# Batch 0's k maximum by TensorE, half of q times kv on another PSUM ring, an uneven last cut, and new lists of order, engines and loads

## The chip, the cores and the metric

The kernel runs on one core of one Trainium2 chip. The metric is the device time of one launch in microseconds, as the median of several runs. 0.2% of it is 0.48 us.

## What is computed

Eight batches of eight heads with 576 tokens and 64 values per head go through "efficient" attention, and the result (4608 tokens of 512 values) through a multiplicative feed-forward network. All arrays are float32.

```
q_s = softmax(q, axis=-1)           # over the 64 values of a token
k_s = softmax(k, axis=2)            # over the 576 tokens; the maximum is over tokens too
kv  = einsum('bhsd,bhse->bhde', k_s, v)          # 64 x 64 for each head
x   = einsum('bhsd,bhde->bhse', q_s, kv)         # transposed to (4608, 512)
out = ((x @ w1) * (x @ w2) @ w3) @ w_out   # 512 -> 1024 -> 1024 -> 512
```

## The kernel before, in words

**The fold.** w3 @ w_out is formed once on the chip as `W3O`, in eight slices `ft`: `w3t` (L445) is eight TensorE transposes of 128x128 into a bank of the PSUM ring "pab", `w3T` copies them to SBUF, `pf.ft.0` and `pf.ft.1` (L457) are four matmuls of 512 columns each with the two halves of w_out (loads `wo.0`, `wo.1`) into a bank of the ring "po", and `W3O.ft` scales the sum out. Slices 4 and 5 share one load `w3.4`, 6 and 7 share `w3.5`; the others have one each (`w3.0` to `w3.3`).

**Attention of a batch b.** q: `qmx` (maximum over a token's values, L582), `qsub` (L587), `qexp` (L595), `qsm` (sum, L600), `qeps`, `qrc` (L612), `qn` (normalized q, fp16, L619), each in two parts of the tokens; then q is transposed, by TensorE (`qt`, L634, and a copy `qT`) in the first batches or by a DMA (`qd`, L642). k: `kmx` (L498 to L501) takes the maximum over a partition's own nine tokens by a tree of DVE operations. The tokens of a head lie over 64 partitions, so the maximum over them comes next: `cba` (a 32x32 stream transpose of DVE, L505, and a reduction, L508), `cbx` (four small ACT copies that bring the other 32 partitions' values across, L514) and `cb` (a reduction, L518, and a transposing spread, L520). `ksub` (L524) subtracts it, `kexp` (L532) takes the exponential. `kv` (L549, L559) multiplies k_s and v, `kve` and `kv2` (L566 to L575) divide by the sums. `xm.b.0`, `xm.b.1` and `xt.b` (L667) multiply q and kv: 512 tokens in two halves of the heads, and the 64 tokens left over; `xs` and `xts` copy them out as x in fp16.

**The network in chunks c.** Chunk c = 0 to 7 has batch c's first 512 tokens, chunk 8 the 8 x 64 left over. `up.1.c.sub.u` and `up.0.c.sub.u` (L784) are four matmuls for x @ w2 and x @ w1 each; `bs` copies the first out of PSUM, `ab` (L799, DVE) multiplies it with the second; `down.c.tb` (L806, eight matmuls of 512 columns) multiplies with `W3O`, `os` copies to SBUF and `st` stores. Chunks 0 and 1 are done in two halves of 256 tokens, and in chunk 0 each load of 256 columns of w1 and w2 is used as it comes. In chunk 8 the last quarter `down.8.3` (L821) is cut in columns, so that its copies and stores begin sooner.

**What sets the order.** Three PSUM rings of banks hold the products: "pab" (4), "po" (2), "att" (2). All steps are written out in the list `ORDER`; each engine executes its own in that order, and waits where data, a bank or a buffer are not there. `PICKS` names the engine for those steps that have a choice. `FILL` names steps ahead of which matmuls on zeros (L352) are put. Loads stand in three lists: `HW` (batch 0's q, on SP's queue), `LOADS` (on POOL's queue, at most eight outstanding: each load waits until the one eight places ahead has landed) and `LATE` (on SP again, after `w1.3` of `LOADS`). The rings and pools are declared so:

```
pab_pool = ctx.enter_context(tc.tile_pool(name="pab", bufs=4, space=bass.MemoryType.PSUM))
po_pool = ctx.enter_context(tc.tile_pool(name="po", bufs=2, space=bass.MemoryType.PSUM))
att_pool = ctx.enter_context(tc.tile_pool(name="att", bufs=2, space=bass.MemoryType.PSUM))
```

Of the kernel before, what the change touches and what calls it, by code (L numbers as in the profile page):

```python
# [10 lines left out]
F32 = mybir.dt.float32  # L11
# [6 lines left out]
class Plan:  # L18
# [59 lines left out]
q.0.1 qmx.0.1 qsub.0.1 qexp.0.1 q.0.0 ident w3.4 w3t.5 qmx.0.0 qsm.0.1 wo.0 wo.1 w3.2 k.0 w3.0 w3.3  # L78
w3.5 w3t.4 w3T.5 w3.1 w3T.4 qeps.0.1 qsub.0.0 qrc.0.1 qexp.0.0 qn.0.1 v.0 pf.5.0 pf.4.0 pf.5.1 w3t.2
qsm.0.0 k.1 w2.0 w3T.2 W3O.5 q.1.0 qt.0.16 qt.0.8 qT.0.8 pf.4.1 qT.0.16 qeps.0.0 qrc.0.0 qn.0.0 w1.0  # L80
pf.2.0 pf.2.1 w3t.0 W3O.2 W3O.4 w3T.0 qt.0.0 w3t.3 pf.0.0 w3T.3 w2.1 pf.0.1 pf.3.0 w3t.7 kmx.0.0
cba.0 cbx.0 w1.1 pf.3.1 W3O.0 w3T.7 w3t.1 pf.7.0 w3t.6 w1.2 w2.2 cb.0 ksub.0.1 ksub.0.0 kexp.0.1
kexp.0.0 pf.7.1 qT.0.0 kv.0 W3O.3 w3T.1 W3O.7 kve.0 pf.1.0 pf.1.1 w3T.6 kv2.0 xm.0.0 pf.6.0 pf.6.1
xs.0.0.1 kmx.1.0 xs.0.0.0 xm.0.1 xs.0.1.0 xs.0.1.1 up.1.0.0.0 bs.0.0.0 xt.0 qmx.1.0 k.2 w2.3 cba.1
cbx.1 up.0.0.0.0 up.1.0.1.0 up.0.0.1.0 W3O.1 bs.0.1.0 ab.0.0.0 up.1.0.0.1 up.0.0.0.1 w1.3 v.1
qsub.1.0 qexp.1.0 q.1.1 q.2 xts.0.0 bs.0.0.1 up.1.0.1.1 ab.0.1.0 cb.1 up.0.0.1.1 up.1.0.0.2 qsm.1.0
ksub.1.1 bs.0.1.1 ab.0.0.1 up.0.0.0.2 up.1.0.1.2 qeps.1.0 xts.0.1 qrc.1.0 qn.1.0 bs.0.0.2 ab.0.1.1
ab.0.0.2 kmx.2.0 cba.2 bs.0.1.2 kexp.1.1 up.0.0.1.2 up.1.0.0.3 up.0.0.0.3 up.1.0.1.3 bs.0.0.3 W3O.6
# [52 lines left out]
ab.8.0.1 st.6.3 os.7.0 os.7.1 down.7.2 up.0.8.0.2 up.1.8.0.3 ab.8.0.2 bs.8.0.3 up.0.8.0.3 up.1.8.0.4
up.0.8.0.4 ab.8.0.3 bs.8.0.4 ab.8.0.4 up.1.8.0.5 bs.8.0.5 up.0.8.0.5 up.1.8.0.6 bs.8.0.6 ab.8.0.5
up.0.8.0.6 ab.8.0.6 up.1.8.0.7 up.0.8.0.7 bs.8.0.7 ab.8.0.7 down.7.3 st.7.0 os.7.2 down.8.0 st.7.1
st.7.2 os.7.3 os.8.0 down.8.1 down.8.2 st.7.3 os.8.1 os.8.2 st.8.0 down.8.3.0 os.8.3.0 down.8.3
os.8.3 st.8.1 st.8.2 st.8.3.0 st.8.3
"""


FILL = {
    "begin": 17, "pf.5.0": 6,  # L150
}


PICKS = {
# [773 lines left out]
```

## Time and profile before

| what | value |
| --- | --- |
| median of 3 runs | 239.51 us (239.41 to 239.68) |
| the profiled execution | 239.21 us |
| its span, first to last instruction | 237.4 us |
| TensorE (PE) busy | 230.1 us, 97% |
| DVE, ACT, POOL busy | 180.3, 121.7, 110.0 us |
| fills (L352) | 23, 8.0 us |
| first up projection starts at | 33.49 us |

The span is that of one profiled execution; the launch's time holds 1.8 us more. Engines are PE (TensorE), PEld (its weight loads), DVE (VectorE), ACT (ScalarE), POOL (GpSimd) and SP (SyncE). Lines name an instruction by its source line, its output and inputs by the program's names. A row of a timeline is start, length, engine, line, operation, count, and in brackets the idle time of the engine ahead of it and what ended it. A row of the waits is engine, tile and line, what was waited for, and the total, count and longest in us. A row of the groups ends in busy time, mean ns of one and the idle time ahead. A row of a table by windows has, after the length, the busy us and the instructions of PE, PEld, DVE, ACT and POOL, then the granted clock, the DMA engines' busy share and GB/s.

### The profile page before, as it was taken

The numbers are of one execution on the slowest core, as the hardware profiler recorded it, in microseconds if no ns is written. First come the engines' busy times: TensorE is split into PE (matmuls) and PEld (weight loads), VectorE is DVE, ScalarE is ACT, GpSimd is POOL, SyncE is SP. The second block draws the span as 40 slices with busy tenths as digits, with TensorE's granted clock in tenths as the row PEclk, the third lists the DMA queues.
The fourth block names the chain that finished last, engine by engine and source line by source line (L and its number), as shares of the span: only waits on it lengthen the run. The fifth ranks groups of instructions, "written<-read, shape, count | busy, mean of one in ns | idle before, by whom it ended". The sixth has DMA issues, their size and how long they took to land.

```text
span 237.4 us, 4860 instructions
## 1 busy us (share of the span) xinstructions
PE 230.1 (97%) x1935; PEld 119.5 (50%) x1935; DVE 180.3 (76%) x277; ACT 121.7 (51%) x221; POOL 110.0 (46%) x73
## 2 busy tenths in 40 slices
PE   7889999999999999999999999999999999999994
PEld 2445658756856444444444444444444444444443
DVE  2998699998998999998999798679566365326640
ACT  1437854499856997777747754258405111010002
POOL 8234258469958899469673593338500000000000
PEclk9999999999999999999999999999999999999999
DMA  6999999999999998959699984250042070163053
GB/s 207 214 307 209 306 245 300 328 299 382 401 226 309 405 217 179 385 132 282 242 113 281 387 338 95 51 135 0 3 91 52 0 179 2 32 145 88 3 132 133
DMA packets 38742, 46.51 MB, mean 196 GB/s; under 512 B 17088, under 2 KB 22976, under 8 KB 38720
## 3 DMA queue, kind: packets, MB, share of 16 engines
q1 hardware_dynamic: 31184, 34.48, 50.2%
q0 software_dynamic: 7536, 11.73, 21.1%
q8 instruction: 15, 0.25, 0.4%
q14 instruction: 7, 0.06, 0.1%
HBM read 38.80 MB, written 9.44 MB: 203 GB/s over the span
## 4 chain that ended last, share of the span: by engine, by line
PE 81%; DMA 8%; DVE 5%; POOL 4%; issue 1%; ACT 0%; POOLq 0%; ACTq 0%
PE pab L784 46%; PE po L806 22%; DMA w<-in_moe_w_dram 6%; PE po L457 4%; PE po L821 3%; PE pkv L549 2%; DMA qT<-en 2%; PE xm L667 1%; DVE qm L582 1%; POOL k L524 1%; PE w3t L445 1%; POOL en L619 1%; POOL w L406 1%; DVE ab L799 1%; DVE kmx L498 1%
## 5 line engine op out<-in xcount | busy, mean ns | idle before, releaser
L784 PE MATMUL pab<-x,w1sb 128*128 128x512 f16 (+1 forms) x320 | 65.9, 337 | 0.4 <-DVE kmx L499 0.4
L784 PE MATMUL pab<-x,w2sb 128*128 128x512 f16 (+1 forms) x320 | 66.0, 337 | 0.0
L799 DVE TENSOR_TENSOR ab<-pab,bsb 128x512 f16<-128x512 f32 x72 | 48.6, 682 | 20.2 <-PE pab L784 13.6
L806 PE MATMUL po<-W3O,ab 128*128 128x512 f16 x256 | 58.9, 379 | 0.0
L784 PEld LDWEIGHTS <-w1sb 128*128 128x128 f16 x352 | 34.2, 98 | 28.5 <-DMA w1sb<-in_moe_w_dram 0.6
L784 PEld LDWEIGHTS <-w2sb 128*128 128x128 f16 x352 | 33.5, 98 | 27.5 <-issue 0.7
L325 ACT CAST bsb<-pab 128x512 f16<-128x512 f32 x46 | 26.8, 582 | 35.8 <-PE pab L784 34.6
L524 POOL TENSOR_TENSOR k<-k,cb 128x1152 f32<-128x1152 f32 x12 | 31.4, 2628 | 16.4 <-issue 5.1
L806 PEld LDWEIGHTS <-ab 128*128 128x128 f16 x256 | 24.5, 98 | 28.5 <-issue 0.4
L587 POOL TENSOR_TENSOR q<-q,qm 128x1024 f32<-128x1024 f32 (+1 forms) x14 | 29.5, 2125 | 13.1 <-DVE rc L573 5.4
L325 ACT COPY osb<-po 128x512 f32<-128x512 f32 (+1 forms) x25 | 14.3, 571 | 40.3 <-PE po L806 26.8
L619 POOL TENSOR_TENSOR en<-eq,qr 128x1024 f16<-128x1024 f16 (+1 forms) x13 | 27.2, 2106 | 10.5 <-DVE qr L612 10.4
L582 DVE TENSOR_REDUCE qm<-q 128x20 f32<-128x1280 f32 (+1 forms) x16 | 21.2, 1340 | 3.6 <-DMA q<-in_q_dram 3.6
L325 DVE CAST bsb<-pab 128x512 f16<-128x512 f32 x26 | 17.6, 677 | 6.8 <-PE pab L784 6.3
L600 DVE TENSOR_REDUCE qr<-eq 128x20 f32<-128x1280 f16 (+1 forms) x16 | 21.5, 1341 | 1.5 <-ACT eq L595 1.4
L595 ACT ACTIVATE eq<-q 128x1280 f16<-128x1280 f32 (+1 forms) x16 | 18.5, 1161 | 4.8 <-DVE q L587 3.9
L532 ACT ACTIVATE ek<-k 128x1152 f16<-128x1152 f32 x16 | 18.2, 1163 | 3.8 <-POOL k L524 3.8
L489 DVE TENSOR_REDUCE km<-k 128x128 f32<-128x1152 f32 x8 | 16.9, 2149 | 0.0
L457 PE MATMUL po<-wosb,w3T 128*128 128x512 f16 x64 | 15.3, 379 | 0.5 <-DMA wosb<-in_moe_w_out_dram 0.5
L325 DVE COPY osb<-po 128x512 f32<-128x512 f32 x12 | 8.3, 688 | 9.1 <-PE po L806 7.9
L329 ACT ACTIVATE x<-xm 128x512 f16<-128x512 f32 x18 | 10.3, 597 | 6.4 <-PE xm L667 6.2
L325 ACT CAST v<-v 128x1152 f16<-128x1152 f32 x9 | 10.3, 1148 | 0.3 <-DMA v<-in_v_dram 0.3
(70 smaller groups left out, 194.0 us busy)
## 6 DMA issues: line engine op xcount, KB each, us to landing
out_dram<-osb SPq DMA_DIRECT2D x66, 128.0 KB, 2.6
q<-in_q_dram SPq DMA_DIRECT2D x5, 1152.0 KB, 7.7
v<-in_v_dram SPq DMA_DIRECT2D x5, 1152.0 KB, 8.9
k<-in_k_dram SPq DMA_DIRECT2D x4, 1152.0 KB, 10.1
k<-in_k_dram POOLq DMA_DIRECT2D x3, 1152.0 KB, 14.1
v<-in_v_dram POOLq DMA_DIRECT2D x1, 1152.0 KB, 13.9
v<-in_v_dram SPq DMA_DIRECT2D x2, 576.0 KB, 5.9
q<-in_q_dram SPq DMA_DIRECT2D x2, 576.0 KB, 7.7
```

The lines of the kernel that those rows point to most:

```text
L325: return [(nc.scalar.copy if eng == "ACT" else engine[eng].tensor_copy)(out=out, in_=in_)]
L457: nc.tensor.matmul(st["pf", ft], lhsT=st["w3T", ft][:, gt, :], rhs=wosb[:, gt, :], start=(gt == 0), stop=(gt == N_FT - 1))
L524: return [engine[eng].tensor_tensor(out=kb[:, two(hp), :, :], in0=kb[:, two(hp), :, :], in1=st["cb", b][:, two(hp), None, :].broadcast_to( ...
L532: nc.scalar.activation(out=st["ek", b][:, hp, :, :].rearrange("p j (i d) -> p i j d", i=2), in_=kb[:, two(hp), :, :], func=AF.Exp)
L582: dve.tensor_reduce(out=st["qm", b][:, :, j], in_=qb[:, :, j, :], axis=AX.X, op=ALU.max)
L587: return [engine[eng].tensor_tensor(out=qb[:, :, j, :], in0=qb[:, :, j, :], in1=st["qm", b][:, :, j, None].broadcast_to([P, HH, n, D]), op ...
L595: nc.scalar.activation(out=st["eq", b, p], in_=qb[:, :, j, :], func=AF.Exp)
L600: dve.tensor_reduce(out=st["qr", b][:, :, slice(*PARTS[p])], in_=st["eq", b, p], axis=AX.X, op=ALU.add)
L619: return [engine[eng].tensor_tensor(out=st["en", b][:, j, :, :].rearrange("p j h d -> p h j d"), in0=st["eq", b, p], in1=st["qr", b][:, :, ...
L784: nc.tensor.matmul(st["p", one, c, sub, u][:, a * (t1 - t0):(a + 1) * (t1 - t0)], lhsT=w[:, ct, fb * P:(fb + 1) * P], rhs=x()[:, ct, t0:t1 ...
L799: dve.tensor_tensor(out=st["ab", c][:, nf * u:nf * u + nf, t0:t1], in0=cut(st["p", 0, c, sub, u]), in1=cut(st["bsb", c, sub, u]), op=ALU.mult)
L806: nc.tensor.matmul(st["po", c, tb], lhsT=st["ab", c][:, ft, tb * P:(tb + 1) * P], rhs=W3O[:, ft, :], start=(ft == 0), stop=(ft == N_FT - 1))
```

## The change

1. `PEK = [0]`: for batch 0 the maximum over partitions is no longer made by `cba`, `cbx`, `cb`. TensorE transposes the partial maxima as float32 (`kT`, two transposes with a float32 identity `ident32`), DVE reduces along the free axis (`kr`), and four float32 matmuls of 128 columns with the identity as the moving operand spread the result over 64 partitions each (`kB`). `ksub.0` reads it from PSUM, on DVE only. Other batches keep the old way.
2. From batch 3 on `xm.b.0` takes its bank from "pab" instead of "att"; `xm.b.1` stays on "po", `xt.b` on "pab".
3. The last block's cut is 320 and 192 columns instead of 256 and 256.
4. `FILL` goes from 17 at the start and 6 ahead of `pf.5.0` to 14 at the start and 8 ahead of `pf.2.0`.
5. `LOADS`, `LATE`, `ORDER` and `PICKS` are listed anew. In `LOADS`, `w3.2` and `w3.0` stand ahead of `wo.0`, and `q.1.0` ahead of `k.1`. The fp16 identity is made on POOL behind the first two loads instead of ahead of them. In `PICKS` some steps change between DVE, ACT and POOL (`qsub.0.0` goes to POOL, `ksub.1.0` to DVE, the last block's 320 columns to DVE).

```diff
 FILL = {
-    "begin": 17, "pf.5.0": 6,
+    "begin": 14, "pf.2.0": 8,
 }
...
 LOADS = [
-    ("w3", 4), ("wo", 0), ("wo", 1), ("w3", 2), ("k", 0), ("w3", 0), ("w3", 3), ("w3", 5),
-    ("w3", 1), ("v", 0), ("k", 1), ("w2", 0), ("q", 1, 0), ("w1", 0), ("w2", 1), ("w1", 1),
-    ("w1", 2), ("w2", 2), ("k", 2), ("w2", 3), ("w1", 3), ("v", 1), ("q", 1, 1),
+    ("w3", 2), ("w3", 4), ("w3", 0), ("wo", 0), ("wo", 1), ("k", 0), ("w3", 3), ("w3", 5),
+    ("w3", 1), ("v", 0), ("q", 1, 0), ("k", 1), ("w1", 0), ("w2", 0), ("w2", 2), ("w2", 1),
+    ("w1", 1), ("w1", 2), ("k", 2), ("w2", 3), ("w1", 3), ("v", 1), ("q", 1, 1),
 ]
...
+    plan.add(("ident32",), "ACT", 0.28, lambda: nc.scalar.copy(out=ident32, in_=ident16), needs=[("ident",)],
+             lead=200.0)
...
+        def kT():
+            st["kT", b] = kbank("kT")
+            for n in range(NHP):
+                nc.tensor.transpose(st["kT", b][:, n, :], st["km", b].rearrange("p h d -> p (h d)")[
+                    :, n * P:(n + 1) * P], ident32)
+
+        def kr():
+            st["kr", b] = work.tile([P, NHP, G], F32, tag="kr", name="kr")
+            dve.tensor_reduce(out=st["kr", b], in_=st["kT", b].rearrange("p n (g r) -> p n g r", g=G),
+                              axis=AX.X, op=ALU.max)
+
+        def kB():
+            st["kB", b] = kbank("kB")
+            for n in range(NHP):
+                for gg in range(G):
+                    nc.tensor.matmul(st["kB", b][gg * HALF:(gg + 1) * HALF, n, :],
+                                     lhsT=st["kr", b][:, n, gg:gg + 1].broadcast_to([P, HALF]),
+                                     rhs=ident32, start=True, stop=True)
+            if not b:
+                st["cb", b] = st["kB", b].rearrange("p n (i d) -> p (n i) d", d=D)
...
-            return "pab" if name[0] == "xt" else "po" if name[2] else "att"
+            return "po" if name[0] == "xm" and name[2] else "pab"
...
+        if b in PEK:
+            A(("kT", b), "PE", 0.45, kT, kms + [("ident32",)], takes=kring)
+            A(("kr", b), "DVE", 0.45, kr, [("kT", b)], gives=[("kT", b)])
+            A(("kB", b), "PE", 0.45, kB, [("kr", b)], takes=kring)
+            cbs, cbg = [("kB", b)], [("kB", b)]
...
-                cuts = [0, C // 2, C] if tb == 3 else [0, C]
+                cuts = [0, 320, C] if tb == 3 else [0, C]
```

On TensorE's list after the change stand, ahead of the first up projection: 14 fills, `w3t.2`, `w3t.4`, `w3t.5`, `w3t.0`, 8 fills, `pf.2.0`, `pf.0.0`, two transposes of q, `pf.2.1`, `pf.0.1`, `pf.5`, the third transpose of q, `pf.4`, `kT`, `w3t.3`, `kB`, `w3t.6`, `w3t.7`, `pf.3`, `w3t.1`, `pf.6`, `kv.0`, `pf.1`, `xm.0.0`, `pf.7`, `xm.0.1`. Before it stood: 17 fills, `w3t.5`, `w3t.4`, 6 fills, `pf.5.0`, `pf.4.0`, `pf.5.1`, `w3t.2`, two transposes of q, `pf.4.1`, `pf.2`, `w3t.0`, the third, `w3t.3`, `pf.0`, `pf.3.0`, `w3t.7`, `pf.3.1`, `w3t.1`, `pf.7.0`, `w3t.6`, `pf.7.1`, `kv.0`, `pf.1`, `xm.0.0`, `pf.6`, `xm.0.1`.

More of the change, by code (lines that the diff above doesn't have):

```diff
@@ L77 @@
 ORDER = """
[L78 to L88, printed above, removed]
@@ L141 @@
[L141 to L145, printed above, removed]
+q.0.1 qmx.0.1 q.0.0 qsub.0.1 w3.2 w3.4 ident w3t.2 qmx.0.0 w3T.2 qexp.0.1 w3.0 wo.0 wo.1 k.0 w3.3
@@ new lines @@
+w3.5 qsub.0.0 qsm.0.1 qexp.0.0 qeps.0.1 w3t.4 w3t.5 w3t.0 w3T.0 qrc.0.1 w3.1 qn.0.1 qsm.0.0 pf.2.0
+pf.0.0 v.0 q.1.0 qt.0.8 qt.0.16 pf.2.1 qeps.0.0 pf.0.1 qT.0.8 qrc.0.0 W3O.2 w3T.5 W3O.0 w3T.4
+ident32 k.1 qn.0.0 pf.5.0 pf.5.1 qt.0.0 pf.4.0 pf.4.1 kmx.0.0 kT.0 kr.0 w3t.3 kB.0 W3O.5 w3T.3 W3O.4
+w1.0 qT.0.0 w3t.6 ksub.0.1 w3T.6 w3t.7 pf.3.0 pf.3.1 kexp.0.1 ksub.0.0 w3t.1 qT.0.16 pf.6.0 W3O.3
+kexp.0.0 pf.6.1 kv.0 w2.0 w2.2 w2.1 w1.1 qmx.1.0 W3O.6 w1.2 k.2 w3T.1 qsub.1.0 kve.0 w3T.7 pf.1.0
+pf.1.1 kv2.0 xm.0.0 pf.7.0 pf.7.1 xs.0.0.1 xs.0.0.0 xm.0.1 w2.3 qexp.1.0 up.1.0.0.0 up.0.0.0.0
@@ L571, in kv2 @@
             st["kv2", b] = work.tile([P, NHP, G, D], F16, tag="kv2", name="kv2")
+            if b not in KVE:
+                st["rc", b] = work.tile([P, G, NHP], F32, tag="rc", name="rc")
+                for gg in range(G):
+                    dve.tensor_scalar_add(out=st["rc", b][:, gg, :], in0=ps[gg][:, :, D], scalar1=EPS)
             rc = st["rc", b]
```

173 lines of the change are left out of this document (105 added, 68 removed), and 107 rows, old and new, of the table PICKS.

## The prediction

> **What bounds the kernel now.** I read the page's first part, then the waits of PE, then PE's timeline up to the first up projection, then the queue that feeds it.
>
> ```profile
> span 237.4 us, 4860 instructions
> PE 230.1 (97%) x1935; PEld 119.5 (50%) x1935; DVE 180.3 (76%) x277; ACT 121.7 (51%) x221; POOL 110.0 (46%) x73
> PE po L352 <- DVE zero L347: 1.6, 1, 1.6
> PE w3t L445 <- DMA w<-in_moe_w_dram: 1.2, 3, 0.8
> PE po L457 <- DMA wosb<-in_moe_w_out_dram: 0.5, 1, 0.5
> PE xm L667 <- DMA qT<-en: 0.5, 1, 0.5
> PE pab L784 <- DVE kmx L499: 0.4, 1, 0.4
> ```
>
> The first two lines are the page's, the others are all that PE waits for. TensorE is the bound: 237.4 − 230.1 = 7.3 us of idle time, and the waits shown are 4.2 us of it, all but 0.9 in the first 20 us; the rest lies behind the last matmul. From 74 us to the end PE has no gap, so all that the re-listed order, engines and queues do there can only lose time, except at the very end. What can be won or lost lies ahead of the first up projection, and PE's timeline shows it:
>
> ```profile
> 1.55 6.53 PE L352 MATMUL po<-zero 128*128 128x512 f16 x17 [1.55 <-DVE zero L347]
> 8.87 1.21 PE L445 MATMUL w3t<-ident,w 128*128 128x128 f16 x16 [0.79 <-DMA w<-in_moe_w_dram]
> 9.91 1.46 PE L352 MATMUL po<-zero 128*128 128x512 f16 x6
> 11.41 1.89 PE L457 MATMUL po<-wosb,w3T 128*128 128x512 f16 x8
> 13.80 1.02 PE L457 MATMUL po<-wosb,w3T 128*128 128x512 f16 x4 [0.50 <-DMA wosb<-in_moe_w_out_dram]
> 15.05 0.71 PE L445 MATMUL w3t<-ident,w 128*128 128x128 f16 x8 [0.23 <-DMA w<-in_moe_w_dram]
> 15.60 0.72 PE L634 MATMUL qtp<-ident,en 128*128 128x128 f16 x10
> 19.13 0.71 PE L445 MATMUL w3t<-ident,w 128*128 128x128 f16 x8 [0.21 <-DMA w<-in_moe_w_dram]
> 27.90 0.78 PE L549 MATMUL pkv<-v,ek 64*64 64x64 f16 x72
> ...
> 33.49 1.05 PE L784 MATMUL pab<-x,w2sb 128*128 128x256 f16 x8
> 45.79 0.39 PE L784 MATMUL pab<-x,w1sb 128*128 128x256 f16 x2 [0.36 <-DVE kmx L499]
> 73.37 0.41 PE L667 MATMUL xm<-qT,kv 64*64 64x512 f16 x4 [0.46 <-DMA qT<-en]
> ```
>
> Each row is start, length, instruction, and in brackets the idle time ahead of it with its releaser. The fold of w3 and w_out (transposes at L445, products at L457) begins when its weights land, and the first up projection comes at 33.49 us, after a chain of 22.08 us from the first product at 11.41.
>
> The weights come down one queue, issued by POOL, with eight loads outstanding. So POOL's timeline tells when a load landed: the ninth load is issued when the first is there, and so on.
>
> ```profile
> 1.44 0.87 POOL L406 DMA_DIRECT2D w<-in_moe_w_dram  x1
> 9.11 0.55 POOL L406 DMA_DIRECT2D w<-in_moe_w_dram  x1 [2.63 <-DMA w<-in_moe_w_dram]
> 11.56 0.75 POOL L406 DMA_DIRECT2D v<-in_v_dram  x1 [1.90 <-DMA wosb<-in_moe_w_out_dram]
> 14.04 0.76 POOL L406 DMA_DIRECT2D k<-in_k_dram  x1 [1.74 <-DMA wosb<-in_moe_w_out_dram]
> 15.29 0.74 POOL L406 DMA_DIRECT2D w2sb<-in_moe_w_dram  x1 [0.48 <-DMA w<-in_moe_w_dram]
> 18.27 0.75 POOL L406 DMA_DIRECT2D q<-in_q_dram  x1 [2.24 <-DMA k<-in_k_dram]
> 19.36 0.74 POOL L406 DMA_DIRECT2D w1sb<-in_moe_w_dram  x1 [0.34 <-DMA w<-in_moe_w_dram]
> 34.76 0.75 POOL L406 DMA_DIRECT2D v<-in_v_dram  x1 [0.51 <-DMA w1sb<-in_moe_w_dram]
> 45.79 0.22 PEld L784 LDWEIGHTS <-w1sb 128*128 128x128 f16 x3 [0.64 <-DMA w1sb<-in_moe_w_dram]
> ```
>
> The issues stand 0.24 us behind the landings (9.11 against PE's start at 8.87, 14.04 against 13.80, 15.29 against 15.05). So w3.4 landed at 8.87, wo.0 at 11.32, wo.1 at 13.80, w3.2 at 15.05, k.0 at 18.03, w3.0 at 19.1, w1.0 at 34.52: one load behind the other, 2.46 us for a long weight load (w3.4, w3.5, wo.0, wo.1) and 1.1 to 1.25 us for a short one. The last row puts the 0.36 us at 45.79, which PE's waits ascribe to the k maximum, on a load: w1.3.
>
> **The change, part by part.** *Loads.* w3.2 and w3.0 now stand ahead of wo.0, so wo.0 lands 1.25 + 1.1 us later, at 13.7, and the first product starts at about 13.8: +2.4 us. In exchange four transposed tiles instead of two are done by then: w3.2 lands at 8.87 − 2.46 + 1.25 = 7.66, w3.4 at 10.1, w3.0 at 11.3, and PE transposes between them. The chain from the first product to the first up projection then loses two groups of transposes (0.55 us each, 15.05 to 15.60: −1.1) and the four waits in it: 0.50, 0.23, 0.21 shown and one of 0.13 (−1.07), since the weights are now there before PE comes to them. It gains the two fp32 steps of the k maximum. No row shows an fp32 matmul. Six of them at the price of a 128-column fp16 transpose (0.55/8 = 0.07 us) are 0.4 us; at the 0.71 us that eight take with nothing behind them, and twice over for twice the bytes, each alone on the engine, 6 × 0.4 = 2.4 us. I take 0.9, the 0.45 us for each step that the change's own list plans, nearer to the transposes since these too stream 128 columns. So 22.08 − 1.07 − 1.1 + 0.9 = 20.8, and the first up projection could start at 13.8 + 20.8 = 34.6, with the bounds of fp32 between 34.1 and 36.1. There is a floor too: it needs w2.0, and ahead of that stand in the new list the same loads that stood ahead of w1.0, which landed at 34.52. So it starts at 34.6, against 33.49: **+1.1** (+1.0 to +2.6).
>
> *What the fold hides.* The new wait of the kT step for the k maximum has the rest of the fold behind it on PE. k.0 has w3.0 ahead of it now and lands at 19.1; the maximum's tree took 2.9 us (rows below), so km is there at 22.0. On PE the products of four tiles (1.8 us each, as 1.89 at 11.41) and 18 transposes of q stand between wo.0's landing and kT: 13.8 + 4 × 1.8 + 18 × 0.06 = 22.1. The cover is 0.1 us, next to none: of what DVE is late, nearly all goes to the end, and all the rest of the fold queues behind it on PE. I take it as on time, since the subtraction of q, 1.2 us of DVE's, goes to POOL ahead of it. w3t.3 lies between kT and kB and covers the reduction of the transposed maximum (0.42, as that of the old way).
>
> ```profile
> 18.43 1.22 DVE L498 TENSOR_TENSOR kmx<-k 128x1024 f32<-128x1024 f32 x1
> 21.32 0.45 DVE L505 STREAM_TRANSPOSE kmq<-km 128x256 f32<-128x256 f32 x1
> ...
> 23.79 2.63 DVE L524 TENSOR_TENSOR k<-k,cb 128x1152 f32<-128x1152 f32 x2
> ```
>
> The way taken out, two stream transposes, two reductions and four ACT copies, took from 21.32 to 23.79, 2.5 us, beside PE's products. Now ksub can start about 1.5 us behind km, but that frees no PE time by itself: kv came at 27.90 with PE busy ahead of it, and by the new order PE is there near 29.5, when ksub (2.63) and the exponentials (2 × 1.2, half beside ksub) from 24.4 on are done at 28.3.
>
> *Given back.* w1.3 has the same loads ahead as before and PE comes to it 1.1 us later: **−0.36**. The product at 73.37 waited 0.46 us for a transpose by DMA of half of batch 2's q; the new order normalizes that half ahead of batch 3's first maximum of q instead of behind both (1.2 us or more on DVE), and PE comes some 0.6 us later: **−0.46**.
>
> *The end.* The last block is cut 320 and 192 instead of twice 256.
>
> ```profile
> L325 ACT COPY osb<-po 128x512 f32<-128x512 f32 x23 | 13.5, 588 | 39.5 <-PE po L806 26.8 <-PE po L821 10.1 <-issue 2.6
> L325 ACT COPY osb<-po 128x256 f32<-128x256 f32 x2 | 0.7, 372 | 0.8 <-PE po L821 0.8
> ```
>
> (588 − 372)/256 = 0.84 ns a column, so 64 columns less behind the last matmul are **−0.05**.
>
> *New stalls.* In the first chunk DVE has no room, and it gets a subtraction of batch 1 that POOL did (half of the 2.63 above), with one copy of the fold taken away:
>
> ```profile
> 34.00:46.00 12.00, 11.64 (x111) 9.81 (x110) 11.60 (x20) 5.91 (x15) 8.13 (x6) 1.00 1.29 286
> ```
>
> DVE is busy (third figure of the engines) 11.60 us of 12, and PE's rings are freed by it. This and the banks of the up projection's ring that half of q times kv takes from batch 3 on, held for a copy of 0.59 us each, cost between 0 and 1 us; I take **+0.3**, since PE lost nothing to DVE in that stretch before.
>
> The fills (17 + 6 before, 14 + 8 now) lie in waits for loads and cost nothing, so long as the clock stays up (below). Sum: 1.1 − 0.36 − 0.46 − 0.05 + 0.3 = +0.5 us. The profiled execution took 239.21 us, so 239.7; it stands 0.3 under the median of the runs, so **240.0**. By its bounds, without a dear fp32 and with new stalls of 0 to 0.9, it is 239.5 to 240.6. 0.2% is 0.48 us, about what a measurement of this kernel can tell from no change.
>
> **The rivals.** *The clock falls back (slower).* The fills keep PE's clock up, and the rows tell what they cost while it is not:
>
> ```profile
> 1.55:3.55 2.00, 2.00 (x5) 0.73 (x6) 1.00 0.72 166
> 6.55:8.08 1.53, 1.53 (x6) 0.45 (x4) 1.00 1.14 216
> ```
>
> At first 5 in 2 us (the granted clock in the row, 1.00, does not show it), then 6 in 1.5, so a slow fill takes some 0.4 us and a fast one 0.24, and the pace is up from 6.55 on. The 17 fills ended at 8.08, the 14 end some 0.7 earlier, at 7.4, and until the 8 fills at 11.9 PE has only 32 transposes (2.2 us) and 2.3 us of idle time. In the trace the stretch from 8.08 to 9.91, idle and transposes alone, left the pace up for the next fills (6 in 1.46); one of 4.5 us it does not show. If the pace falls, the 8 fills take 8 × 0.4 = 3.2 us, to 15.1 instead of 13.8, and the products behind them some 0.2 more: +1.5, 241.5 in all. The Trainium skill (TensorE: Matmul & The Clock Gate, Part 1) has the clock halved after an idle window of about 3.4 us, and Part 4 says that transposes don't count as busy in the same way; by that rule this rival would be the outcome, and the trace neither bears it out nor refutes it, since its longest such stretch is shorter. Chance 0.13.
>
> *fp32 is dear, or kT comes late (slower).* At 1.6 to 2.4 us for the six, or DVE 0.7 to 1.5 us late with km: +0.7 to +1.5 on the sum, 240.7 to 241.5. For it speaks that the tree began 0.4 us behind its load before (18.43 against 18.03), against it that the load comes 1.1 us later now. Chance 0.12.
>
> *The stream starts earlier (faster).* The identity no longer stands ahead of the first load on POOL, which is thus issued some 0.7 us earlier (1.44 to about 0.75), with a short load first.
>
> ```profile
> q1 hardware_dynamic: 1055, 1.18, 63.6%
> q0 software_dynamic: 28, 0.06, 5.0%
> 2.00:4.00 2.00, 2.00 (x6) 0.71 (x5) 0.00 (x0) 0.00 (x0) 2.00 (x5) 1.00 0.86 244
> 4.00:6.00 2.00, 2.00 (x6) 0.76 (x5) 0.88 (x1) 0.83 (x1) 2.00 (x4) 1.00 1.11 368
> ```
>
> In the first 6 us POOL's queue (q0) moved 0.06 MB, though its first load was issued at 1.44, and SP's (q1) the whole of q: against the sum's assumption speaks that 244 GB/s from 2 to 4 us leave room for 0.25 MB, just w3.2. If that fills it, all later loads land up to 1.25 us earlier, the first up projection starts at 33.4, and the sum is −0.1 − 0.87 + 0.3 = −0.7 (w1.3 and the transpose are ahead of PE then too): 238.8, or 238.5 without new stalls. It decides from about 1.0 us, that is the first transposes at 6.6 or sooner. The Trainium skill (DMA: Bandwidth & Descriptors, Queues, rings and completion order) says that an engine takes the queues in turn, packet by packet; the two queue rows here, where one waits until the other is done, do not agree. Chance 0.32, a little of it (0.04) within 0.2%.
>
> **How the numbers follow.** The forecast has 0.43; of its span 239.5 to 240.6, 0.18 lies within 0.2% and 0.25 above. With 0.13 and 0.12 of the slower rivals, slower has 0.50; faster 0.28; within 0.2% 0.22. The range goes from 238.5, the low end of the earlier stream, to 241.9, the clock's 241.5 with some 0.4 us of new stalls more; what lies outside, fp32 at its bound with late maxima and a still earlier stream, I give 0.15. The forecast's own range is 239.5 to 240.6.
>
> **What would show it.** Right: first product at 13.8, kT and kB together under 1 us, first up projection at 34.5 to 34.7, no gap at w1.3 and none at the product of batch 1 near 74. Wrong: first transposes before 7 us (faster), the 8 fills 0.4 us apart (clock), kT and kB over 1.5 us, or idle time of PE behind DVE past 36 us of more than 0.5 us.

## The result, and the profile after

The changed kernel takes 240.69 us (median of 6 runs, 240.34 to 241.35), the kernel before 239.69 us beside it (6 runs): a ratio of 1.0051, 95% interval 1.0039 to 1.0064, so 0.9 to 1.5 us slower (1.0 by the two medians, 1.2 by the ratio). The profiled execution took 240.59 us, its span is 238.8 us, 1.4 us longer than before. The forecast was 240.0 us and slower; the result lies in its range (238.5 to 241.9) and just above the 239.5 to 240.6 that the forecast had as its own.

The waits of PE after the change. All that PE waited for in the middle of the run before (w_out, the transposed q, the 0.36 us at 45.79) is gone; one line is new, the last.

```profile
PE w3t L457 <- DMA w<-in_moe_w_dram: 2.2, 2, 1.8
PE po L362 <- DVE zero L357: 1.6, 1, 1.6
PE pab L857 <- DVE ab L872: 0.8, 1, 0.8
```

PE's timeline after the change, up to the network's first chunk (line numbers are the changed kernel's: L362 fills, L457 transposes of w3, L469 products of the fold, L547 `kT`, L559 `kB`, L857 up projection):

```profile
1.55 5.60 PE L362 MATMUL po<-zero 128*128 128x512 f16 x14 [1.55 <-DVE zero L357]
7.55 0.71 PE L457 MATMUL w3t<-ident,w 128*128 128x128 f16 x8 [0.41 <-DMA w<-in_moe_w_dram]
10.03 2.78 PE L457 MATMUL w3t<-ident,w 128*128 128x128 f16 x24 [1.76 <-DMA w<-in_moe_w_dram]
12.60 2.23 PE L362 MATMUL po<-zero 128*128 128x512 f16 x8
14.67 1.89 PE L469 MATMUL po<-wosb,w3T 128*128 128x512 f16 x8
...
22.77 0.41 PE L547 MATMUL kT<-ident,km 128*128 128x128 f32 x2
23.01 0.65 PE L457 MATMUL w3t<-ident,w 128*128 128x128 f16 x8
23.69 0.66 PE L559 MATMUL kB<-ident,kr 128*64 128x128 f32 x8
24.28 1.21 PE L457 MATMUL w3t<-ident,w 128*128 128x128 f16 x16
...
34.96 1.05 PE L857 MATMUL pab<-x,w2sb 128*128 128x256 f16 x8
...
48.42 1.03 PE L857 MATMUL pab<-x,w2sb 128*128 128x256 f16 x8 [0.77 <-DVE ab L872]
...
74.66 0.41 PE L725 MATMUL xm<-qT,kv 64*64 64x512 f16 x4
```

The first up projection starts at 34.96 instead of 33.49: +1.47. The wait of 0.36 us at 45.79 and that of 0.46 at 73.37 no longer occur; a wait of 0.77 at 48.42 does. 1.47 − 0.36 + 0.77 − 0.46 = 1.42, and the 40 matmuls of the last block start 1.48 us later than before, at 228.89 instead of 227.41 (chain of the change's run):

```profile
228.89 6.94 PE po L894 x40
...
235.89 0.32 ACT osb L335
```

The last copy took 0.32 instead of 0.37 us. The sum of the waits is rough, since an idle time is counted from the modelled end of the matmul ahead of it. From start to start, the product of batch 2 near 74 comes 1.29 us later (74.66, 73.37), and the last block 1.48, so 0.19 us more are lost between the two. No gap shows it: between 76 and 225 us PE is busy throughout in both kernels. The first row is after's, the second before's, each with length and PE's busy time first:

```profile
76.00:225.00 149.00, 149.00 (x1116) 68.98 (x1114) 114.43 (x175) 69.53 (x129) 63.54 (x31) 1.00 0.55 152
```

```profile
76.00:225.00 149.00, 149.00 (x1110) 69.22 (x1110) 112.55 (x170) 73.88 (x135) 63.39 (x30) 1.00 0.56 156
```

Two things in the head call for a reason. The 24 transposes from 10.03 on take 2.57 us to the next fill, 107 ns each, where eight took 0.55 us, 69 ns each, before. A table by windows (the figure behind POOL's is the granted clock) tells why:

```profile
6.45:9.87 3.42, 1.41 (x11) 0.68 (x9) 3.38 (x5) 1.27 (x1) 1.07 (x2) 1.00 1.12 209
9.87:13.28 3.41, 3.25 (x26) 2.87 (x27) 1.68 (x2) 1.26 (x2) 3.30 (x4) 0.50 1.10 217
13.28:14.67 1.39, 1.39 (x8) 0.59 (x7) 1.28 (x3) 0.00 (x0) 0.70 (x1) 1.00 1.10 221
```

The granted clock was 0.50 from 9.87 to 13.28 us, behind a stretch as long in which PE was busy for 1.41 us only. And the loads (POOL's timeline, each row 0.24 us behind a landing):

```profile
13.97 0.76 POOL L416 DMA_DIRECT2D k<-in_k_dram  x1 [0.80 <-DMA wosb<-in_moe_w_out_dram]
...
34.84 0.75 POOL L416 DMA_DIRECT2D v<-in_v_dram  x1 [0.59 <-DMA w2sb<-in_moe_w_dram]
```

wo.0 landed at 13.73, but its first product started at 14.67, since PE was behind with transposes and fills at half the clock; w2.0 landed at 34.60, and the first up projection started 0.36 us later.

The new wait is on DVE (its timeline):

```profile
42.55 0.69 DVE L872 TENSOR_TENSOR ab<-pab,bsb 128x512 f16<-128x512 f32 x1
43.97 1.23 DVE L510 TENSOR_TENSOR kmx<-k 128x1024 f32<-128x1024 f32 x1 [0.73 <-DMA k<-in_k_dram]
...
47.35 0.42 DVE L520 TENSOR_REDUCE mx<-kmq 128x8 f32<-128x256 f32 x1
47.68 1.28 DVE L872 TENSOR_TENSOR ab<-pab,bsb 128x512 f16<-128x512 f32 x2
```

DVE, which works in order, stands idle 0.73 us for batch 2's k, then forms its partial maximum (`kmx.2.0`, `cba.2`, 3.7 us), and only then the product `ab.0.0.2` that frees the bank for which PE waits at 48.42. In the kernel before, the same maximum stood behind `ab.0.0.2` (the second of the two products in the first row) and began at nearly the same time, without an idle DVE ahead of it:

```profile
42.46 1.28 DVE L799 TENSOR_TENSOR ab<-pab,bsb 128x512 f16<-128x512 f32 x2
43.80 1.23 DVE L498 TENSOR_TENSOR kmx<-k 128x1024 f32<-128x1024 f32 x1
```

### The profile page after: what moved, and what is told of

Its sections match the earlier page's. It is cut to its first block, busy times and chain, and to the rows that moved or that the text cites. A ratio compares the mean times of both kernels' runs of the same rounds, so it can differ in the third digit from the quotient of the medians.

```text
span 238.8 us, 4874 instructions
## 1 busy us (share of the span) xinstructions
PE 231.3 (97%) x1944; PEld 120.8 (51%) x1944; DVE 181.3 (76%) x278; ACT 117.2 (49%) x213; POOL 109.6 (46%) x74
## 4 chain that ended last, share of the span: by engine, by line
PE 94%; DMA 3%; issue 0%; DVE 0%; POOL 0%; ACT 0%; ACTq 0%; POOLq 0%
PE pab L857 53%; PE po L879 23%; PE po L469 6%; DMA w<-in_moe_w_dram 3%; PE po L894 3%; PE pkv L603 2%; PE w3t L457 2%; PE xm L725 1%; PE po L362 1%; PE pab L725 1%; PE po L725 1%; PE qtp L692 1%; DVE ab L872 0%; PE kB L559 0%; PE xt L725 0%
## 5 line engine op out<-in xcount | busy, mean ns | idle before, releaser
L857 PE MATMUL pab<-x,w2sb 128*128 128x512 f16 (+1 forms) x320 | 66.0, 337 | 0.8 <-DVE ab L872 0.8
L857 PE MATMUL pab<-x,w1sb 128*128 128x512 f16 (+1 forms) x320 | 65.9, 337 | 0.0
L872 DVE TENSOR_TENSOR ab<-pab,bsb 128x512 f16<-128x512 f32 x72 | 48.1, 683 | 15.9 <-PE pab L857 9.5
L335 ACT CAST bsb<-pab 128x512 f16<-128x512 f32 x43 | 25.0, 586 | 58.8 <-PE pab L857 58.6
L857 PEld LDWEIGHTS <-w2sb 128*128 128x128 f16 x352 | 33.6, 98 | 29.2 <-issue 2.4
L857 PEld LDWEIGHTS <-w1sb 128*128 128x128 f16 x352 | 34.0, 98 | 27.5 <-issue 0.4
L578 POOL TENSOR_TENSOR k<-k,cb 128x1152 f32<-128x1152 f32 x11 | 28.8, 2631 | 12.5 <-DVE k L578 9.9
L677 POOL TENSOR_TENSOR en<-eq,qr 128x1280 f16<-128x1280 f16 (+1 forms) x13 | 27.7, 2141 | 11.7 <-ACT eq L653 6.5
L335 DVE CAST bsb<-pab 128x512 f16<-128x512 f32 x29 | 19.8, 684 | 9.6 <-PE pab L857 9.4
L335 ACT COPY osb<-po 128x512 f32<-128x512 f32 (+1 forms) x27 | 15.4, 577 | 21.3 <-PE po L879 11.3
L335 DVE COPY osb<-po 128x512 f32<-128x512 f32 (+1 forms) x10 | 6.6, 665 | 14.2 <-PE po L879 5.7
L469 PE MATMUL po<-wosb,w3T 128*128 128x512 f16 x64 | 15.1, 380 | 0.0
L335 POOL CAST v<-v 128x1152 f16<-128x1152 f32 x7 | 8.0, 1147 | 7.0 <-PE pab L857 7.0
L362 PE MATMUL po<-zero 128*128 128x512 f16 x22 | 7.8, 528 | 1.6 <-DVE zero L357 1.6
```

Of the source, the lines that this page charges most:

```text
L335: return [(nc.scalar.copy if eng == "ACT" else engine[eng].tensor_copy)(out=out, in_=in_)]
L469: nc.tensor.matmul(st["pf", ft], lhsT=st["w3T", ft][:, gt, :], rhs=wosb[:, gt, :], start=(gt == 0), stop=(gt == N_FT - 1))
L578: return [engine[eng].tensor_tensor(out=kb[:, two(hp), :, :], in0=kb[:, two(hp), :, :], in1=st["cb", b][:, two(hp), None, :].broadcast_to( ...
L677: return [engine[eng].tensor_tensor(out=st["en", b][:, j, :, :].rearrange("p j h d -> p h j d"), in0=st["eq", b, p], in1=st["qr", b][:, :, ...
L857: nc.tensor.matmul(st["p", one, c, sub, u][:, a * (t1 - t0):(a + 1) * (t1 - t0)], lhsT=w[:, ct, fb * P:(fb + 1) * P], rhs=x()[:, ct, t0:t1 ...
L872: dve.tensor_tensor(out=st["ab", c][:, nf * u:nf * u + nf, t0:t1], in0=cut(st["p", 0, c, sub, u]), in1=cut(st["bsb", c, sub, u]), op=ALU.mult)
```

## The experiments

The theory with which I went in: three bounds follow each other in the head, the clock (first product 0.9 us late), the landing of w2.0 (first up projection not before 34.6), and the landing of k.2 with the chain on DVE behind it (48.42). If so, what is won at one is lost at the next. The rival: the fallen clock is the loss, and DVE's own load the wait.

**a_fill: the clock kept up.**

```diff
-    "begin": 14, "pf.2.0": 8,
+    "begin": 14, "w3t.4": 8, "pf.2.0": 8,
```

> The changed kernel with 8 fills more, ahead of w3t.4, so that PE is not idle from 8.3 to 10.0. Theory A (three bounds in a row: clock, then the landing of w2.0, then DVE held by batch 2's k maximum): the granted clock stays 1.00, the 24 transposes of w3.4 and w3.0 take 1.6 us instead of 2.6, the first product starts at 13.8 instead of 14.67, the first up projection at 34.6 (w2.0 lands there) instead of 34.96, and the wait of PE for a product of DVE at 48.42 grows from 0.77 to 1.1, since the landing of k.2 sets its end: time as the changed kernel's, within 0.15 us. Theory B (the fallen clock is the cost): 0.4 to 0.9 us faster than the changed kernel.

Measured: 240.66 us, 1.0042 of before (1.0028 to 1.0056), the changed kernel's time. Its windows and waits:

```profile
10.47:12.26 1.79, 1.75 (x24) 1.62 (x25) 1.05 (x1) 0.69 (x1) 1.79 (x3) 1.00 1.15 228
```

```profile
PE pab L857 <- DVE ab L872: 0.7, 1, 0.7
PE pab L857 <- DMA w2sb<-in_moe_w_dram: 0.4, 1, 0.4
```

The clock is 1.00, the same 24 transposes take 1.8 us, and the first product stands 6.29 us behind the first transposes (7.93, 14.22) instead of 7.12. PE now waits 0.36 us for w2.0, and 0.7 for DVE still. In this run the loads came later than in the run above (the first transposes at 7.93 instead of 7.55, and the first up projection, right behind the landing of w2.0, at 35.19 instead of 34.96), so that positions, not landings, have to be compared; the 34.6 and the wait of 1.1 that theory A gave did not come. So the clock did fall, and keeping it up won 0.8 us at the first product and nothing at the end that the two intervals can tell (1.0042 and 1.0051 of before).

**a_dve, a_both, a_w2: batch 2's maximum behind two products, alone, with the fills, and with w2.0 ahead of w1.0 too.**

```diff
-... kmx.2.0 kexp.1.0 bs.0.0.2 up.1.0.0.3 kexp.1.1 cba.2 qn.1.0 bs.0.1.2 ab.0.0.2 ab.0.1.2 cbx.2 ...
+... kexp.1.0 bs.0.0.2 up.1.0.0.3 kexp.1.1 qn.1.0 bs.0.1.2 ab.0.0.2 ab.0.1.2 kmx.2.0 cba.2 cbx.2 ...
```

> The changed kernel with batch 2's maximum of k (kmx.2.0, cba.2) behind the products ab.0.0.2 and ab.0.1.2 in the order instead of ahead of them. Theory A: the wait at 48.42 goes, the first up projection stays at 34.96, 0.6 to 0.8 us faster than the changed kernel, some 0.4 us slower than the kernel before. Theory B: DVE has no room in that stretch anyway, the wait moves to the next product or to batch 2's kv: within 0.2 us of the changed kernel.

> Both edits, the fills and the order on DVE. Theory A: first product 13.8, first up projection 34.6, no wait at 48: 1.0 to 1.2 us faster than the changed kernel, within 0.2 us of the kernel before. Theory B: the gains of the two add to 0.9 or less and come from the fills alone.

> Both edits, and the load of w2.0 ahead of that of w1.0, one short load (1.3 us) earlier. Theory A: the landing of w2.0 was the floor of the first up projection at 34.6; now PE's own chain of 20.3 us from the first product at 13.8 sets it, 34.1, and the time falls by another 0.4 to 0.5 us, to some 0.4 us under the kernel before. Rival: the floor only moves to w1.0 or to the copies of x, no change against the kernel with both edits.

All three missed: 245.35 us (1.0227 of before, 1.0200 to 1.0253), 244.50 (1.0187, 1.0152 to 1.0222) and 244.08 (1.0167, 1.0123 to 1.0211). The wait at 48.42 is gone, but the third product `ab.0.0.3` still stood behind the rest of batch 2's maximum, which was now later. PE's timeline of a_dve:

```profile
54.54 0.60 PE L879 MATMUL po<-W3O,ab 128*128 128x512 f16 x2 [3.30 <-DVE ab L872]
55.08 1.18 PE L603 MATMUL pkv<-v,ek 64*64 64x65 f16 x72
56.19 4.78 PE L879 MATMUL po<-W3O,ab 128*128 128x512 f16 x16
```

0.77 us became 3.30, and behind it the clock fell again (windows of the same run):

```profile
54.54:56.19 1.65, 1.65 (x75) 1.16 (x75) 1.65 (x2) 1.12 (x3) 1.65 (x1) 0.68 1.03 384
56.19:60.90 4.71, 4.71 (x25) 1.76 (x18) 4.07 (x7) 3.62 (x6) 4.19 (x3) 0.75 0.80 291
```

a_w2 shows one thing cleanly: with w2.0 one load earlier and the clock up, the first up projection came at 34.47, without a wait for w2.0. The floor is the load list's.

**a_ord and a_best: the order mended more carefully; a_best has the fills and w2.0 first as well.**

```diff
-... kmx.2.0 ... cba.2 qn.1.0 bs.0.1.2 ab.0.0.2 ab.0.1.2 cbx.2 up.0.0.0.3 bs.0.0.3 q.2 cb.2 ksub.2.0 ... ab.0.0.3 down.0.0 ...
+... ab.0.0.2 kmx.2.0 ... bs.0.1.2 ab.0.1.2 cba.2 up.0.0.0.3 bs.0.0.3 cbx.2 ab.0.0.3 q.2 cb.2 ksub.2.0 ... down.0.0 ...
-... vc.1.1 qmx.1.1 bs.0.1.3 ab.0.1.3 ...
+... vc.1.1 bs.0.1.3 ab.0.1.3 qmx.1.1 ...
```

> The changed kernel with the order of chunk 0's end mended more carefully: ab.0.0.2 ahead of batch 2's maximum of k, ab.0.1.2 between its tree and its stream transpose, ab.0.0.3 ahead of the rest of it (cb.2, ksub.2.0), bs.0.1.3 and ab.0.1.3 ahead of a maximum of q. The same work on DVE, none taken away. Theory A (the wait at 48.42 is only DVE's order): it goes, and no wait takes its place: 0.6 to 0.8 us faster than the changed kernel, some 0.3 us slower than before. Theory B (DVE has no room there): a wait of like size behind it, time within 0.2 us of the changed kernel.

> The same mended order, with the 8 fills more ahead of w3t.4 and w2.0 loaded ahead of w1.0. Theory A: first product 13.8, first up projection 34.1 to 34.5, no wait at 48: 1.2 to 1.6 us faster than the changed kernel, 0.2 to 0.5 us faster than before. Theory B: PE's lead of 0.5 to 0.9 us runs into DVE or a load again and gains 0.3 us at most over a_ord.

Measured: 242.50 (1.0127, 1.0105 to 1.0149) and 241.53 us (1.0081, 1.0067 to 1.0096), slower than the changed kernel, against both expectations. PE's waits, the same lines in both runs:

```profile
PE pab L857 <- ACT x L339: 1.2, 1, 1.2
PE pkv L603 <- ACT v L335: 1.1, 2, 0.6
```

There is no wait at 48 any more. But batch 2's maximum is later by 1.9 us in a_ord and 1.1 in a_best (the end of `cba.2` starts at 49.24 and 48.49 instead of 47.35), ACT's small copies for it with it, and behind them on ACT stand the casts of batch 1's v for which kv.1 waits, and the copies of x. a_best's first up projection was at 34.31, 0.65 us ahead of the changed kernel's, and it still ended later.

**a_vc: a_best with ACT's order changed for those two waits.**

```diff
-... bs.0.0.3 cbx.2 ... vc.1.0 vc.1.1 bs.0.1.3 ... kexp.2.1 xm.1.0 ... qexp.1.1 xs.1.0.1 xs.1.0.0 ...
+... bs.0.0.3 vc.1.0 vc.1.1 cbx.2 ... bs.0.1.3 ... xm.1.0 ... xs.1.0.1 xs.1.0.0 kexp.2.1 qexp.1.1 ...
```

> As a_best, with the two casts of batch 1's v (vc.1.0, vc.1.1) ahead of batch 2's small copies (cbx.2) on ACT, and the exponentials kexp.2.1 and qexp.1.1 behind the copies of x (xs.1.0). In a_best PE lost 1.08 us to those casts and 1.19 to those copies, at 51 and 59. Theory A (each wait is ACT's order, none its load): both go, 1.5 to 2.2 us faster than a_best, 239.4 to 240.0, about as before. Theory B (batch 2's k is late by now, so the wait moves on to batch 2's kv near 63): at most 1.0 us faster than a_best.

Measured: 244.09 us (1.0199, 1.0175 to 1.0222), a miss worse than theory B. The waits moved on to the next steps:

```profile
PE xm L725 <- DVE kv L633: 1.3, 1, 1.3
PE pkv L603 <- POOL v L335: 1.3, 1, 1.3
...
PE po L879 <- DVE ab L872: 0.8, 1, 0.8
PE pkv L603 <- ACT v L335: 0.4, 1, 0.4
```

So in the three orders tried, the wait went, larger, to whoever stands behind. What was open was what sets it: the load or DVE's work.

**a_pool: less work on DVE.**

```diff
-    "ksub_1_0": "DVE"
+    "ksub_1_0": "POOL"
```

> The changed kernel with batch 1's subtraction ksub.1.0 back on POOL, where the kernel before has it: 1.35 us taken from DVE at 39.0, nothing else. Theory A (the wait at 48.42 is the landing of k.2 at 43.7 and the chain on DVE behind it, kmx.2.0, cba.2, ab.0.0.2): DVE waits 1.35 us longer for k.2, the wait stays at 0.77, time within 0.15 us of the changed kernel. Theory B, as the prediction had it (DVE has no room in that stretch because it got this subtraction): the wait goes or shrinks, 0.4 to 0.8 us faster.

Measured: 241.06 us (1.0060, 1.0047 to 1.0073), not faster than the changed kernel (1.0051, 1.0039 to 1.0064; the intervals overlap). 1.35 us less on DVE, and the wait is as it was; DVE had idle time ahead of the maximum all the same (0.84). The row puts it down to POOL's subtraction, which ended at 44.34. The load was late too: k.2, issued at 30.02 and 13.8 us to its landing, was there at 43.8, about 0.5 us ahead of the maximum, as in the changed kernel (issued at 29.65, landed at 43.5, maximum at 43.97). The trace of this run can't tell the two apart.

```profile
PE pab L857 <- DVE ab L872: 0.8, 1, 0.8
```

```profile
44.37 1.23 DVE L510 TENSOR_TENSOR kmx<-k 128x1024 f32<-128x1024 f32 x1 [0.84 <-POOL k L578]
```

**a_k2: the load earlier.**

```diff
-    ("w1", 1), ("w1", 2), ("k", 2), ("w2", 3), ("w1", 3), ...
+    ("w1", 1), ("k", 2), ("w1", 2), ("w2", 3), ("w1", 3), ...
```

> The changed kernel with one pair of loads swapped: k.2 ahead of w1.2, so that it lands about one short load (1.3 us) earlier, near 42.5, and w1.2 where k.2 did, near 43.5. Nothing else moves, DVE's order least of all. Theory A (the wait at 48.42 is set by k.2's landing and the DVE chain queued behind it): batch 2's maximum starts as soon as DVE is free, at 43.2 instead of 43.97, and the wait shrinks from 0.77 to 0.0 to 0.3; PE waits 0.3 to 0.4 for w1.2 instead, near 43.1, and of that the later wait is shorter once more: 0.3 to 0.5 us faster than the changed kernel. Theory B (the wait comes from DVE's work, not from the load): the wait stays at 0.6 or more, and the time is the same or, by the wait for w1.2, up to 0.4 us longer.

Measured: 240.54 us (1.0050, 1.0037 to 1.0062), the changed kernel's time; the mechanism as theory A had it, the sum not. DVE's and PE's timelines:

```profile
43.15 0.69 DVE L872 TENSOR_TENSOR ab<-pab,bsb 128x512 f16<-128x512 f32 x1
43.76 1.22 DVE L510 TENSOR_TENSOR kmx<-k 128x1024 f32<-128x1024 f32 x1
```

```profile
35.33 1.05 PE L857 MATMUL pab<-x,w2sb 128*128 128x256 f16 x8
...
48.20 1.03 PE L857 MATMUL pab<-x,w2sb 128*128 128x256 f16 x8 [0.18 <-DVE ab L872]
```

DVE goes from the product to the maximum without a gap, and from the first up projection to the matmul that waits it is 12.87 us instead of 13.46: 0.59 less, the difference of the two waits. PE did not wait for w1.2. But in this run the clock fell later and stood longer over the fills, 0.61 from 12.21 to 15.05 (the row of its windows below), and the first up projection was at 35.33, 0.37 later. By that alone the wait, if it ended at 48.42 as in the changed kernel, would be 0.40; the earlier load takes it to 0.18, which is DVE's own work. So the wait at 48.42 is mostly the landing of k.2 with 3.7 us of DVE behind it (DVE's 0.73 us of idle time for it in the changed kernel say the same), and not DVE's load as such; that the time then falls by 0.4 us was not shown.

```profile
12.21:15.05 2.84, 2.84 (x10) 1.11 (x9) 2.48 (x4) 0.24 (x2) 1.75 (x3) 0.61 1.06 212
```

**a_nopek and b_pek: TensorE's way for the k maximum, taken out and put in alone.** a_nopek is a_best with the old way, b_pek the kernel before with the new one:

```diff
 b_pek, on the kernel before
-... w3T.3 w2.1 pf.0.1 pf.3.0 w3t.7 kmx.0.0 cba.0 cbx.0 ... cb.0 ksub.0.1 ...
+... w3T.3 w2.1 kmx.0.0 kT.0 kr.0 pf.0.1 kB.0 pf.3.0 w3t.7 ... ksub.0.1 ...
 a_nopek, on a_best
-    PEK = [0]
+    PEK = []
-... kT.0 kr.0 w3t.3 kB.0 ...
+... cba.0 cbx.0 w3t.3 cb.0 ...
```

> As a_best, but batch 0's k maximum by the old way (two stream transposes, two reductions, four ACT copies; kT, kr, kB gone; the fp32 identity is still made). If the TensorE way only costs PE its 0.84 us: the first up projection 0.8 us earlier, or 0.3 to 0.6 where the landing of w2.0 (33.3) or the copies bound it, and the time that much lower. If it buys anything by its shorter way to ksub (1.6 us from km instead of 2.5): kv.0 comes late by up to 0.9 us less the slack that it has (1.1 us in the changed kernel, from the end of the exponential at 28.9 or less to kv at 29.36), so within 0.3 us of a_best or slower.

> The kernel before with the first part of the change alone: batch 0's k maximum by kT, kr, kB, with kT behind pf.0.0 and kB behind pf.0.1 on PE; loads, fills, cuts, rings and the rest of the order as before. PE has 0.84 us more to do ahead of the first up projection (kT 0.24, kB 0.60 in the changed kernel), so that starts at 34.3 instead of 33.5. Theory A: then the wait of 0.36 us for w1.3 at 45.8 goes, and up to 0.46 at 73.4 with it; 0.0 to 0.5 us slower than before. Theory B: TensorE's way pays, since DVE and ACT get 1.4 and 0.8 us back: faster by 0.2 us or more.

a_nopek took 241.95 us (1.0100, 1.0085 to 1.0116) against a_best's 1.0081 (1.0067 to 1.0096): the intervals overlap, and PE waited 0.2 us for batch 0's exponential and 0.4 for a copy of the fold, in an order written for the new way, so this run decides nothing. b_pek is the cleaner one: 239.59 us, 0.9996 of before (0.9983 to 1.0009), no difference. PE's timeline of b_pek:

```profile
22.40 0.38 PE L541 MATMUL kT<-ident,km 128*128 128x128 f32 x2
22.62 1.03 PE L463 MATMUL po<-wosb,w3T 128*128 128x512 f16 x4
23.58 0.66 PE L553 MATMUL kB<-ident,kr 128*64 128x128 f32 x8
24.17 1.04 PE L463 MATMUL po<-wosb,w3T 128*128 128x512 f16 x4
...
34.78 1.05 PE L851 MATMUL pab<-x,w2sb 128*128 128x256 f16 x8
...
73.89 0.41 PE L719 MATMUL xm<-qT,kv 64*64 64x512 f16 x4
```

`kT` (0.22 to the next row) and `kB` (0.59) cost PE 0.81 us, and the two waits of before, 0.36 and 0.46, are gone. A wait of 0.34 us for a cast of batch 1's v is new (at 53.11). In all, from the first product (11.96, before 11.41) to the product of batch 2 (73.89, before 73.37) it is 61.93 us instead of 61.96: what PE spent was waiting time that it had further on.

**b_xm: the kernel before with the cut of the last block and one matmul group moved.**

```diff
-                cuts = [0, C // 2, C] if tb == 3 else [0, C]
+                cuts = [0, 320, C] if tb == 3 else [0, C]
-... ab.1.1.0 xm.2.0 xs.2.0.0 bs.1.1.1 xs.2.0.1 cbx.3 ab.1.1.1 cb.3 up.1.1.1.2 ...
+... ab.1.1.0 bs.1.1.1 cbx.3 ab.1.1.1 cb.3 up.1.1.1.2 xm.2.0 xs.2.0.0 xs.2.0.1 ...
```

(The 320 columns' copy goes to DVE, as in the change.)

> The kernel before with two small edits alone: the last block cut 320 and 192 with the first copy on DVE (the change's own), and xm.2.0 with its copies behind up.1.1.1.2 in the order, so that PE has 0.87 us of work while the transposed q is on its way. Theory: the wait of 0.46 us at 73.37 goes, the last copy takes 0.32 instead of 0.37 us: 0.3 to 0.5 us faster than before. Rival: up.1.1.1.2 waits for a bank instead, and the gain is the 0.05 us of the end, not to be told from none.

Measured: 238.87 us, 0.9975 of before (0.9961 to 0.9989), faster than both kernels, and at 0.6 us by the ratio (0.3 to 0.9) as much as expected or a little more. The wait at 73.37 is not there any more:

```profile
72.62 1.04 PE L784 MATMUL pab<-x,w2sb 128*128 128x256 f16 x8
73.58 0.41 PE L667 MATMUL xm<-qT,kv 64*64 64x512 f16 x4
```

From the start of the up projection ahead of it to the product it is 0.96 us here and was 1.50 in the run before (71.87 to 73.37): the wait cost 0.54 us, and 0.05 come from the cut.

The ring change of q times kv (part 2) was not tried by itself: the written order of either kernel takes its own rings for granted. Neither was the new list of loads as a whole. The rows from 76 to 225 us show no wait that the ring made. But from the product of batch 2 near 74 to the last block PE has the same steps in both kernels, and they take 154.04 us in the kernel before and in b_pek, and 154.2 to 154.4 in the changed kernel, a_fill, a_pool and a_k2. So rings, order and engines together lose 0.2 to 0.4 us there, in steps too small for a row; which of them does is open.

## Why the prediction was right, and where a term was off

The direction and the place were right; the move was forecast as +0.5 us and measured as +1.0 by the medians (0.9 to 1.5 by the ratio). Step by step:

- *Loads.* wo.0 was forecast at 13.7 and landed at 13.73. The floor of the first up projection, w2.0 in the place of w1.0, was forecast at 34.5 and landed at 34.60. a_fill (a wait of 0.36 us there) and a_w2 (no wait, 34.47) show that it is one.
- *First product at 13.8: 14.67.* Here the clock rival, to which I gave 0.13, took place: 0.50 for 3.4 us. I had priced it at 1.5 on the first product, as 8 fills of 0.4 us, and passed that on whole to the end. It was 0.9 there, and from the 24 transposes (107 instead of 69 ns each), while the 8 fills took 2.07 us in all; of that w2.0's landing left 0.36 at the first up projection, and k.2's landing nothing that a_fill could show at the end. The mechanism had a chance too low and a price too high, because I let it pass two landings that stood in my own rows.
- *The window of the clock.* The Trainium skill (TensorE: Matmul & The Clock Gate, Part 1) has the clock halved after an idle window of about 3.4 us, free-running. The trace agrees in the length, 3.41 us at 0.50; but the stretch ahead of the fall, 6.45 to 9.87, was not idle: it held 0.70 us of fills and 0.71 of transposes, and the gap at its end, to 10.03, was 1.76 us. In a_k2 1.59 us of transposes in the 3.42 us from 7.62 did not keep the clock up either. The Trainium skill (the same page, Part 4) has transposes not counted as busy in the same way. That is not what the changed kernel's rows show: with 0.70 us of fills and 0.71 of transposes the clock fell, and with 0.68 and 2.78 from 9.87 to 13.28 it came back, so the transposes made the difference, as far as one pair of stretches can say.
- *kT and kB.* Forecast 0.9 us with bounds from 0.4 to 2.4, measured 0.24 + 0.59 = 0.83. The chain from the first product to the first up projection was forecast at 20.8 and is 20.29. So the first up projection, forecast at 34.6 and found at 34.96, is near by two errors that offset each other: a first product 0.87 us late and a chain 0.5 us too long. kT was forecast to find km just ready, and did: no wait at 22.77.
- *Given back.* −0.36 and −0.46, both as forecast. The reason that I gave for the second, q normalized ahead of a maximum on DVE, was not looked into; that PE comes later is enough for it, as b_pek shows, whose order there is before's.
- *New stalls, the term that failed.* Forecast +0.3 in all, from DVE having no room and a subtraction more, and from the ring. It is 0.77 in one place, and a_pool, without that subtraction, has the same 0.8; the 0.2 to 0.4 us past 74 us come on top. The step of the prediction that failed is the reading of DVE's 11.60 busy us of 12 as a lack of room. The rows of the order that mattered are those of `kmx.2.0`, now ahead of `ab.0.0.2` while k.2 still lands near 43.5: first of all a load in front of a queue, not the length of the queue. That DVE and ACT have little room all the same, the waits of 1.2 to 3.3 us in the other orders show.
- *The end.* −0.05, measured 0.37 to 0.32.
- *The earlier stream* (0.32) did not come: the first load was issued at 1.25 instead of 1.44, and w3.2 landed at 7.55, where the forecast had 7.66.

With 0.77 for 0.3 and 0.36 for the clock's remainder, the prediction's own sum gives 1.47 − 0.36 − 0.46 − 0.05 + 0.77 = 1.37, the 1.4 of the two spans. That it fits so well is in part luck: from start to start the waits weigh otherwise, and 0.19 us of the 1.4 lie past 74 us.

## What to carry to other kernels

When a head is bound by a stream of loads, write down every landing that PE or an engine in front of it must pass; a cost ahead of a landing is paid only by what it exceeds it, and a gain there is lost the same way. For an engine that works in order, look at which of its instructions waits for a load, and what stands behind it: changing that order by hand moved a wait of 0.77 us to steps behind it and made it 1.2 to 3.3 us. A single wait that ends in an idle PE, with independent work next in the list (b_xm), is the cheap case.

## What the runs showed that I had not expected

- Four fp32 matmuls stand in the trace as eight records, 74 ns apart (`kB`: 0.59 us for x8), while an fp32 transpose is one record (`kT`: x2 in 0.24 us).
- A wait of PE of 3.1 to 3.3 us can make the clock fall or not: it fell behind 3.30 us in a_dve and 3.11 in a_w2, and not behind 3.31 in a_both. The kernel a_both took 242.90 us in the run with a mean granted clock of 1.000, and 245.46 in the one with 0.986: one program, and up to 2.6 us between its executions; the first of the two was profiled.
- In the changed kernel the mean granted clock and the time go together too, but weakly: 240.34 us at 0.993, 241.35 at 0.986. In a_pool two runs at 1.000 (240.93, 241.09) are not faster than two at 0.993 (241.05, 241.07): there, what the clock takes ahead of a landing costs nothing that shows at the end.
